# A buffer for x's second part, a later start for pairs 3 to 10, and w_out's sums in thirds of one tile

## The chip, the cores and the metric

One core of a Trainium2 chip. The metric is the device time of one execution, in microseconds; lower is better.

## What is computed

```python
q_n, k_n = rmsnorm(q, g_q), rmsnorm(k, g_k)            # q, k, v: 8 batches x 12 heads x 448 x 64
scores = q_n @ k_n.T / sqrt(64);  scores -= scores.max(-1)
attn = exp(scores) / (exp(scores).sum(-1) + 1e-9)
x = heads_side_by_side(attn @ v)                       # 3584 x 768
h = x @ w_in                                           # 768 x 2048
g = s * maximum(h, 0) ** 2 + b
return g @ w_out                                       # 2048 x 768, result 3584 x 768, float32
```

The weights arrive as 64-bit words; the kernel makes float32 of them itself.

## The kernel before

**Order.** Every engine runs its instructions in the order in which the program issues them: a block switches the scheduler off for all engines, so the order is written by hand. SP issues nearly all DMAs, one after the other; a DMA that waits for a buffer or for data holds up all that stands behind it on SP.

**Attention** works on 48 pairs of heads. A pair has four pieces, each a slot (192 slots, and negative ones for the start). `slot(i)` issues the scores and the maxima due there, the transposed scores and the exponent of piece i, and then a list of jobs. `STAGES` (L30) says in which slot a pair's jobs are issued: an offset, and a tuple with the slots of the first pairs. The jobs: `load` brings raw q and k rows (L192, 448 KB, two buffers, on SP for pairs 0 to 3, on ACT's queue later); `norm` squares on ACT (L198), sums on DVE (L203, ssq), and takes the power −1/2 on POOL (L205, L206, ri); `keep` writes these factors to memory (L209, i_d); `load_kq` brings k, q and v (L215, kqv, 704 KB); `spread` reads i_d back as a broadcast (L222, rb, two buffers); `scale` multiplies by g on ACT (L229) and by rb on POOL (L233, DVE for half of pair 0), and three slots later casts to kr (ACT L238). Then `score` (PE L247, sh), `maximum` (DVE L256, nmx), `shift` (SP L265, shq), `score_t` (PE L276, and L280 with shq), `exponent` (ACT L287, e), `weigh` (PE L297, L304) and `take` (ACT L319, L320). A tail per pair fetches the sums (L323, L327), inverts them (L331), writes them (L336, z_d), reads them as a broadcast (L341, uz), divides on POOL (L347) and writes x (L350). `convert` brings w_in's words (L356) and makes float32 sums of them on the side.

**FFN.** Both products are done in blocks of 2 x 2 with seven products of sums instead of eight. x is read in parts: `s_load` (SP L449) into a tile of nine (tag s9, two pools of one buffer each), `s_sums` (POOL L137 to L139), `s_split` (ACT cast L149, DVE subtraction L151) into tags s0, s1, s2. Three parts, s_0 to s_2, are needed by the first product, `ffn_in` (PE L483, 63 matmuls a block, 56 blocks n); they are issued among attention's last slots, in program order for SP, POOL, ACT and DVE alike. `rectify` empties a block's banks (ACT L494 to L497, DVE L492) and writes r_d (L527). Beside blocks 2 to 50, `convert_out` makes sums of w_out in 32 steps, two for each k from 0 to 15: a load (L575), the words (ACT L110, DVE L111 to L118), sums on POOL; `keep_out` writes w_d (L593). The sums stand in a tile of nine, odd k under 12 in a pool with two buffers (w9), all others in a single buffer (o9). `tout_load` (L560) brings seven of them back, two buffers from w9; `tout_split` (L149, L151) makes the high and the low part for the last stage, `multiply` (PE L657).

```python
            if k % 2 and k < 12:
                o9s[k] = pools["w9"].tile([P, 9, HC], F32, tag="w9", bufs=2, name=f"o9_{k}")
            else:
                o9s[k] = pools["c"].tile([P, 9, HC], F32, tag="o9", name=f"o9_{k}")
```

Of the kernel before, what the change touches and what calls it, by code (L numbers as in the profile page):

```python
# [9 lines left out]
F32 = mybir.dt.float32  # L10
# [17 lines left out]
AHEAD = 10  # L28

STAGES = {  # L30
    "raw": (-21, (-14, -14, -12, -11, -8, -5, -2, 0, 2)),
    "norm": (-16, (-13, -12, -10, -7, -4, -1, 1, 3)),
    "keep": (-13, (-11, -9, -7, -4, -2, 1, 3)),
    "kq": (-8, (-12, -8)),
    "spread": (-10, (-10, -9, -6, -3, 0, 2)),
    "scale": (-5, (-9, -5, -2, 1, 3, 6)),
}


# [6 lines left out]
def attention_then_relu2_ffn(  # L46
# [17 lines left out]
    NPAIR, P, _, TILES, D = kq_rows.shape  # L64
# [10 lines left out]
    NSLOT = W * NPAIR  # L75
# [17 lines left out]
    HC = HALF // 2  # L93
    TG = 4 * P
    NG = NT // TG
    QUADS = 4
# [70 lines left out]
    def attention(ps):  # L167
# [212 lines left out]
        def at(slot, f, *a):  # L380
            jobs[slot].append((f, a))
# [15 lines left out]
            at(s0 + 20, put_x, p)  # L397
        at(FIRST, constants)
        for n in range(NM * NK):
            at(8 + 27 * n // 4, convert, n)  # L400

        def slot(i):
            if i == FIRST:
# [36 lines left out]
    def s_load(n):  # L440
        u, k = divmod(n, NK)
        g = min(u, 2 * NG - 2 - u)
        t = s9s[n] = pools["s9", n % 2].tile([P, 9, 2 * P], F32, tag="s9", name=f"s9_{n}")
        t0 = TG * g
        while t0 < TG * (g + 1):
            b, off = divmod(t0, SEQ)
            w = min(TG * (g + 1) - t0, SEQ - off)
            o = t0 - TG * g
            nc.sync.dma_start(  # L449
                four(t, 2 * P)[:, :, o : o + w],  # L450
                x_d[b][2 * k : 2 * k + 2, :, off : off + w].rearrange("f p t -> p f t"),
            )
            t0 += w
# [10 lines left out]
    def finish(g):  # L464
        for _ in g:
            pass
# [95 lines left out]
    def tout_split(k):  # L562
        m, h = divmod(k, 2)
        to, c = t_out(m), slice(h * HC, (h + 1) * HC)
        return split((to[:, 0, :, c], to[:, 1, :, c]), tls.pop(k))

    o9s = {}

    def convert_out(n):
        k, nh = divmod(n, 2)  # L570
        m, h = divmod(k, 2)
        w = pools["c"].tile([P, 2, HC, 2], I32, tag="c64", bufs=2, name=f"w64o{n}")
        c0 = 2 * (nh * HALF + h * HC)
        src = w_out32[2 * m * P : 2 * (m + 1) * P, c0 : c0 + 2 * HC]
        nc.sync.dma_start(  # L575
            w.rearrange("p h n t -> p h (n t)"), src.rearrange("(h p) n -> p h n", h=2)
        )
        yield
        if nh == 0:
            if k % 2 and k < 12:  # L580
                o9s[k] = pools["w9"].tile([P, 9, HC], F32, tag="w9", bufs=2, name=f"o9_{k}")
            else:
                o9s[k] = pools["c"].tile([P, 9, HC], F32, tag="o9", name=f"o9_{k}")
        t = o9s[k]
        yield from words_of(
            t[:, nh : nh + 8 : 7].bitcast(I32), (w[:, :, :, 0], w[:, :, :, 1]),
            t[:, 2 + 2 * nh : 4 + 2 * nh],
        )
        if nh:
            sums_right(t, G)  # L590
# [100 lines left out]
    with tc.manual_schedule(engines=ORDERED):  # L691
        lp = ctx.enter_context(tc.tile_pool(name="lpool", bufs=1))
        ap = early.enter_context(tc.tile_pool(name="apool", bufs=1))
        aps = early.enter_context(tc.tile_pool(name="aps", bufs=1, space=PSUM))
        slot = attention(aps)
        for i in range(FIRST, NSLOT + 3):
            slot(i)
            if i == NSLOT - 10:
                first.close()
                pools["s", True] = pools["s9", 0] = pools["s9", 1] = pool(mid, "spool", "right")  # L700
            for n in range(NK):
                if i == NSLOT - (10, 9, 6)[n]:
                    s_load(n)
                if i == NSLOT - (8, 6, 4)[n]:
                    s_sums(n)
                if i == NSLOT - (7, 5, 3)[n]:
                    finish(s_split(n))
        early.close()
        pools["w9"] = pools["t4"] = pool(ctx, "w9pool", "left")
        pools["c"] = pools["s9", 1] = pool(late, "cpool2", "left")  # L710
        pools["s", False] = pool(mid, "spool2", "right")
        ps = ctx.enter_context(
            tc.tile_pool(name="ps", bufs=1, space=PSUM, reuse_waits="tile")
        )
        todo = list(range(4 * NM))
        runs = [(g, 0) for g in range(NG)] + [(g, QUADS) for g in reversed(range(NG))]
        blocks = [(r, g, q0 + i) for r, (g, q0) in enumerate(runs) for i in range(QUADS)]
        nb = len(blocks)

        def fresh_x(r):  # L720
            return r + 1 < len(runs) and r != NG - 1

        def sums(n):

            r, _, q = blocks[n]
            if fresh_x(r):
                for k in {1: (0, 1), 2: (2,)}.get(q % QUADS, ()):
                    s_sums(first_s(r + 1) + k)

        def parts(n):  # L730

            r, _, q = blocks[n]
            if fresh_x(r):
                for k in {1: (0,), 3: (1, 2)}.get(q % QUADS, ()):
                    finish(s_split(first_s(r + 1) + k))
            b = n - (NG - 1) * QUADS
            if -2 <= b <= 0:
                for k in range(2):
                    tin_load(2 * (b + 2) + k)
            if 0 < b <= QUADS:  # L740
                for k in range(NK):
                    finish(tin_split(NK * (b - 1) + k))
                    tin_load(NK * (b + 1) + k)
            if n == nb - 14:
                tout_load(0)
                tout_load(1)
            if n == nb - 13:
                finish(tout_split(0))
                finish(tout_split(1))
            b = n - (nb - QUADS)  # L750
            if b == 0:
                tout_load(2)
                tout_load(3)
            elif b > 0:
                for k in (2 * b, 2 * b + 1):
                    finish(tout_split(k))
                    tout_load(k + 2)

        for n, (r, g, q) in enumerate(blocks):
            ffn_in(r, q)  # L760
            i = q % QUADS
            if fresh_x(r):
                for k in {0: (0, 1), 2: (2,)}.get(i, ()):
                    s_load(first_s(r + 1) + k)
            last, next_ = begun[:], []
            begun.clear()
            if n >= 2 and todo and i != 2 and not 24 <= n < 28:
                x = todo.pop(0)
                c = convert_out(x)
                next(c)  # L770
                next_.append(c)
                if x % 2 and x > 1:
                    keep_out(x // 2 - 1)
            sums(n)
            if n:
                rectify(*blocks[n - 1])
            for u in range(3 * n, 3 * n + 3):
                if u < 20:
                    slot(NSLOT + 3 + u)
            for x in last:  # L780
                finish(x)
            begun.extend(next_)
            parts(n)
            if n == nb - QUADS - 1:
                assert not todo and not begun
                keep_out(2 * NM - 1)
                late.close()
                pools["g"] = pool(ctx, "gpool", "left")
                for x in range(3):
                    g_load(x)  # L790
            if n == nb - 3:
                g_sums(0)
                g_sums(1)
            if n == nb - 2:
                g_load(3)
                g_load(4)
        g_split(0)
        mid.close()
        pools["t"] = pool(ctx, "tpool", "right")
        rectify(*blocks[-1])  # L800
        g_split(1)
        g_sums(2)
        for k in (8, 9):
            finish(tout_split(k))
            tout_load(k + 2)
        for x in range(ROUNDS):
            g_load(x + 5)
            g_sums(x + 3)
            p, m = divmod(x, NM)
            if m < NM - 1:  # L810
                g_split(x + 2)
            for k in {0: (10, 11), 1: (12,), 2: (13,), 3: (14,), 4: (15,)}.get(x, ()):
                finish(tout_split(k))
                if k < 14:
                    tout_load(k + 2)
            if x < ROUNDS - 2:
                multiply(x)
            elif x == ROUNDS - 1:
                multiply(x - 1, x)
            if m == NM - 1:  # L820
                combine(p)
                g_split(x + 2)
            if m == 1 and p:
                store(p - 1)
# [42 lines left out]
```

## Time and profile before

| | |
|---|---|
| median of three runs | 1416.88 us (1413.33 to 1419.38) |
| the profiled execution, time | 1416.61 us |
| its span | 1414.8 us |
| TensorE (PE) busy | 1342.3 us, 95% |
| VectorE (DVE) | 1001.4 us, 71% |
| ScalarE (ACT) | 779.5 us, 55% |
| GpSimd (POOL) | 824.1 us, 58% |
| mean granted clock of TensorE | 0.978 |

Attention takes the span's first 558 us, the first product runs to about 987, the second to the end. In each, TensorE is busy almost throughout; its idle time is gathered at the start, between the stages, and at a few places inside.

### The profile page before, as it was taken

The numbers are of one execution on the slowest core, as the hardware profiler recorded it, in microseconds if no ns is written. First come the engines' busy times: TensorE is split into PE (matmuls) and PEld (weight loads), VectorE is DVE, ScalarE is ACT, GpSimd is POOL, SyncE is SP. The second block draws the span as 40 slices with busy tenths as digits, with TensorE's granted clock in tenths as the row PEclk, the third lists the DMA queues.
The fourth block names the chain that finished last, engine by engine and source line by source line (L and its number), as shares of the span: only waits on it lengthen the run. The fifth ranks groups of instructions, "written<-read, shape, count | busy, mean of one in ns | idle before, by whom it ended". The sixth has DMA issues, their size and how long they took to land.

```text
span 1414.8 us, 25920 instructions
## 1 busy us (share of the span) xinstructions
PE 1342.3 (95%) x9760; PEld 1068.7 (76%) x9760; DVE 1001.4 (71%) x1539; ACT 779.5 (55%) x1185; POOL 824.1 (58%) x714
## 2 busy tenths in 40 slices
PE   3699999999999996999999999899899999999999
PEld 2344444444444443999999999899799999999998
DVE  3467767776666631789888886777977766777666
ACT  3467767766666652333435332435665665656654
POOL 5468988877878623656544445260455655455553
PEclk6799999999999998999999999999999999999999
DMA  6578898889899813556567566457533332233231
GB/s 212 163 194 228 243 234 257 233 256 263 239 268 262 238 57 113 177 188 207 183 230 251 173 199 207 160 186 248 200 98 110 107 98 90 90 118 99 98 96 61
DMA packets 170733, 252.12 MB, mean 178 GB/s; under 512 B 53680, under 2 KB 121200, under 8 KB 170608
## 3 DMA queue, kind: packets, MB, share of 16 engines
q1 hardware_dynamic: 164272, 230.29, 52.7%
q10 hardware_dynamic: 6336, 20.19, 5.2%
q8 instruction: 76, 1.25, 0.4%
q14 instruction: 49, 0.40, 0.1%
HBM read 181.49 MB, written 68.76 MB: 177 GB/s over the span
## 4 chain that ended last, share of the span: by engine, by line
PE 74%; DMA 8%; DVE 6%; issue 4%; POOL 3%; ACT 3%; SPq 1%; ACTq 0%; DVEq 0%; POOLq 0%
PE m L657 27%; PE h L483 21%; PE av L297 9%; PE st L276 8%; PE av L304 4%; PE sh L247 4%; DMA uz<-z_d 2%; PE st L280 2%; DMA to<-w_d 2%; DVE r L492 1%; DMA i_d<-ri 1%; DVE s L151 1%; DVE nmx L256 1%; ACT s L149 1%; DMA w_d<-o 1%
## 5 line engine op out<-in xcount | busy, mean ns | idle before, releaser
L483 PE MATMUL h<-s,tin 128*128 128x256 f32 x3528 | 423.8, 283 | 5.4 <-DVE r L492 4.2
L483 PEld LDWEIGHTS h<-s,tin 128*128 128x128 f32 x3528 | 422.1, 190 | 8.0 <-DVE r L492 5.7
L657 PE MATMUL m<-tout,gh 128*128 128x384 f32 x1568 | 403.3, 338 | 3.3 <-ACT gh L641 3.1
L256 DVE TENSOR_REDUCE nmx<-sh 112x2 fp32r<-112x896 f32 x192 | 209.1, 1090 | 144.3 <-PE sh L247 141.4
L657 PEld LDWEIGHTS m<-tout,gh 128*128 128x128 f32 x1568 | 285.8, 189 | 4.7 <-ACT gh L641 3.7
L657 PE MATMUL m<-tout,gl 128*128 128x384 f32 x784 | 265.7, 339 | 5.0 <-DVE gl L642 5.0
L287 ACT ACTIVATE e<-st 128x896 f32<-128x896 f32 x192 | 176.7, 922 | 118.1 <-PE st L280 117.8
L621 POOL TENSOR_TENSOR g<-g 128x256 f32<-128x256 f32 x112 | 94.6, 845 | 218.7 <-DVE g L620 218.7
L276 PE MATMUL st<-kqv 64*128 64x448 f32 x768 | 181.6, 550 | 8.3 <-ACT e L287 8.3
L642 DVE TENSOR_TENSOR gl<-g,gh 128x896 fp32r<-128x896 f32 x112 | 138.1, 1233 | 62.6 <-ACT gh L641 62.4
L297 PE MATMUL av<-e,kqv 128*32 128x448 f32 x1536 | 166.2, 551 | 11.2 <-ACT uz L320 7.2
L641 ACT CAST gh<-g 128x896 fp32r<-128x896 f32 x112 | 105.5, 942 | 111.2 <-POOL g L625 59.9
L657 PEld LDWEIGHTS m<-tout,gl 128*128 128x128 f32 x784 | 148.4, 189 | 6.9 <-DVE gl L642 6.9
L233 POOL TENSOR_TENSOR kqv<-kqv,rb 128x448 f32<-128x448 f32 x95 | 122.7, 1306 | 49.6 <-ACT kqv L229 19.6
L492 DVE TENSOR_TENSOR r<-r,h 128x256 f32<-128x256 f32 x408 | 139.4, 413 | 12.6 <-ACT r L496 12.4
L280 PE MATMUL st<-shq,row 64*128 64x448 f32 x384 | 141.0, 726 | 4.8 <-DMA shq<-nmx 4.8
L247 PEld LDWEIGHTS sh<-kr 64*112 64x112 f32 x384 | 54.4, 278 | 115.9 <-issue 29.3
L206 POOL TENSOR_TENSOR ri<-ri,mhalf 128x14 f32<-128x14 f32 x48 | 138.9, 2893 | 4.0
L625 POOL TENSOR_TENSOR g<-g 128x256 f32<-128x256 f32 x112 | 135.6, 1211 | 0.0
L151 DVE TENSOR_TENSOR s<-s,s 128x1792 fp32r<-128x1792 f32 x39 | 82.0, 2108 | 57.1 <-ACT s L149 56.6
L247 PE MATMUL sh<-kr 64*112 64x448 f32 x384 | 92.5, 478 | 29.4 <-ACT kr L238 19.7
L149 ACT CAST s<-s 128x1792 fp32r<-128x1792 f32 x39 | 66.0, 1696 | 81.0 <-POOL s L139 48.1
(78 smaller groups left out, 1604.2 us busy)
## 6 DMA issues: line engine op xcount, KB each, us to landing
kqv<-in_dram SPq DMA_DIRECT2D x48, 704.0 KB
raw<-r_d SPq DMA_DIRECT2D x112, 256.0 KB
r_d<-r SPq DMA_DIRECT2D x51, 512.0 KB
rb<-i_d SPq DMA_DIRECT2D x96, 224.0 KB
raw<-in_dram ACTq DMA_DIRECT2D x44, 448.0 KB
w64i<-in_dram SPq DMA_DIRECT2D x24, 512.0 KB
w64o<-in_dram SPq DMA_DIRECT2D x32, 384.0 KB
uz<-z_d SPq DMA_DIRECT2D x96, 112.0 KB
```

What stands on the lines that cost most here:

```text
L206: G.tensor_tensor(ri, ri, mhalf[:, :n], ALU.pow)
L247: T.matmul(sh[:QC, j, :SEQ], t[d, 1].rearrange("k (p c) -> k c p", c=NQ)[:, c], t[d, 0], start=True, stop=True,)
L256: V.tensor_reduce(out=nmxs[p][:, :, c : c + 1], in_=shs.pop(i)[:QC, :, :SEQ], op=ALU.max, axis=AX.X, negate=True,)
L276: T.matmul(st[:, j, :SEQ], t[d, 0, k0 : k0 + P], t[d, 1], start=True, stop=False)
L280: T.matmul(st[:, j, :SEQ], row[d], shq[p % 3][d], start=False, stop=True)
L287: S.activation(e, sts.pop(i)[:, :, :SEQ], AF.Exp)
L297: T.matmul(t[n * Q : (n + 1) * Q, 0, :SEQ], x[:, 2 * g + h, j, m * Q : (m + 1) * Q], e[h][:, j], start=g + h == 0, stop=g + h == 2,)
L483: T.matmul(to, w[:, lw, sa], x[:, lx, tb], start=k == n == 0 and j % 2 == 0, stop=k == NK - 1 and n == 2, skip_group_check=True,)
L492: V.tensor_tensor(to, a, part(j), op_)
L625: G.tensor_tensor(g9[:, 5:7], g9[:, 0:9:8], g9[:, 1:8:6], ALU.subtract)
L642: V.tensor_tensor(gl, g9[:, 1:8], gh.bitcast(F32), ALU.subtract)
L657: T.matmul(to, g[:, sa], w, start=m == 0 and n == 0, stop=m == NM - 1 and n == 2,)
```

## The change

Three parts. **The start:** `STAGES` issues the kqv of pair 0 before the second raw, and moves load, powers, i_d and rb of pairs 3 to 10 to later slots; w_in's conversions begin in slot 14 instead of 8, the last begins in slot 163 as before. **The end of attention:** s_load(1) uses the place of tag s2, where the result of part 2 will go, instead of the s9 buffer that part 0 used; loads, sums and splits of parts 1 and 2 are issued in other slots. **w_out:** for k from 8 on, the sums stand in one of three thirds of a tile `spare`, which takes the place (tag t0) that `staged` had and `tout0` will have; below 8, odd k use w9 and even ones o9. The first two tout loads move from block 42 to block 50, their splits from 43 to 52.

```diff
 STAGES = {
-    "raw": (-21, (-14, -14, -12, -11, -8, -5, -2, 0, 2)),
-    "norm": (-16, (-13, -12, -10, -7, -4, -1, 1, 3)),
-    "keep": (-13, (-11, -9, -7, -4, -2, 1, 3)),
-    "kq": (-8, (-12, -8)),
-    "spread": (-10, (-10, -9, -6, -3, 0, 2)),
-    "scale": (-5, (-9, -5, -2, 1, 3, 6)),
+    "raw": (-21, (-14, -14, -12, -9, -5, 0, 2, 4, 6, 8)),
+    "norm": (-16, (-13, -12, -10, -2, -1, 2, 4, 6, 8, 10)),
+    "keep": (-13, (-11, -9, -7, 0, 2, 4, 6, 9, 11)),
+    "kq": (-8, (-14, -12, -6, -1, 1, 3)),
+    "spread": (-10, (-10, -8, -6, 0, 3, 4, 7, 10)),
+    "scale": (-5, (-9, -4, -2, 1, 4, 6)),
 }
...
-            at(8 + 27 * n // 4, convert, n)
+            at(14 + 13 * n // 2, convert, n)
...
-        t = s9s[n] = pools["s9", n % 2].tile([P, 9, 2 * P], F32, tag="s9", name=f"s9_{n}")
+        tag = "s2" if n == 1 else "s9"
+        t = s9s[n] = pools["s9", n % 2].tile([P, 9, 2 * P], F32, tag=tag, name=f"s9_{n}")
...
-            if k % 2 and k < 12:
+            if k >= 8:
+                if not spare:
+                    spare.append(pools["t4"].tile([P, 3, 9, HC], F32, tag="t0", name="spare"))
+                o9s[k] = spare[0][:, k % 3]
+            elif k % 2:
...
-                if i == NSLOT - (10, 9, 6)[n]:
+                if i == NSLOT - (10, 9, 5)[n]:
                     s_load(n)
-                if i == NSLOT - (8, 6, 4)[n]:
+                if i == NSLOT - (8, 6, 3)[n]:
                     s_sums(n)
-                if i == NSLOT - (7, 5, 3)[n]:
+                if i == NSLOT - (7, 4, 1)[n]:
                     finish(s_split(n))
...
-            if n == nb - 14:
+            b = n - (nb - QUADS)
+            if b == -2:
                 tout_load(0)
                 tout_load(1)
-            if n == nb - 13:
-                finish(tout_split(0))
-                finish(tout_split(1))
-            b = n - (nb - QUADS)
-            if b == 0:
-                tout_load(2)
-                tout_load(3)
-            elif b > 0:
+            if b >= 0:
                 for k in (2 * b, 2 * b + 1):
                     finish(tout_split(k))
                     tout_load(k + 2)
```

What moves at the start, on SP, from its first transfer to the first shift. A number behind a name counts the program's tiles; raw_373 is pair 0's in both, i_d_275 to i_d_279 belong to pairs 0 to 4. Before:

```order
L192 DMA raw_373<-in_dram 128x896
L192 DMA raw_375<-in_dram 128x896
L157 DMA gg<-in_dram 128x2
L215 DMA kqv_385<-in_dram 128x1408
...
L215 DMA kqv_427<-in_dram 128x1408
L222 DMA rb_429<-i_d_277 64x896 x2
L209 DMA i_d_278<-ri_424 128x14
L215 DMA kqv_453<-in_dram 128x1408
L222 DMA rb_455<-i_d_278 64x896 x2
L209 DMA i_d_279<-ri_450 128x14
L265 DMA shq_343<-nmx_440 1x112x4 x2
```

After:

```order
L192 DMA raw_373<-in_dram 128x896
L215 DMA kqv_375<-in_dram 128x1408
L192 DMA raw_377<-in_dram 128x896
L157 DMA gg<-in_dram 128x2
...
L209 DMA i_d_277<-ri_404 128x14
L215 DMA kqv_419<-in_dram 128x1408
L222 DMA rb_421<-i_d_277 64x896 x2
L265 DMA shq_343<-nmx_429 1x112x4 x2
```

gg stands behind a kqv as well, and the first shift stands directly behind the rb of pair 2, no longer behind i_d, kqv and rb of pair 3 and i_d of pair 4.

On DVE the same stretch, before:

```order
L203 TENSOR_REDUCE ssq_402<-raw_388 128x14
L233 TENSOR_TENSOR kqv_385<-kqv_385,rb_398 128x448
L203 TENSOR_REDUCE ssq_422<-raw_396 128x14
L256 TENSOR_REDUCE nmx_440<-sh_437 112x2
L256 TENSOR_REDUCE nmx_440<-sh_444 112x2
L203 TENSOR_REDUCE ssq_448<-raw_416 128x14
L256 TENSOR_REDUCE nmx_440<-sh_458 112x2
L256 TENSOR_REDUCE nmx_440<-sh_470 112x2
```

After:

```order
L203 TENSOR_REDUCE ssq_402<-raw_390 128x14
L233 TENSOR_TENSOR kqv_375<-kqv_375,rb_398 128x448
L256 TENSOR_REDUCE nmx_429<-sh_426 112x2
L256 TENSOR_REDUCE nmx_429<-sh_434 112x2
L256 TENSOR_REDUCE nmx_429<-sh_438 112x2
L256 TENSOR_REDUCE nmx_429<-sh_446 112x2
L203 TENSOR_REDUCE ssq_452<-raw_411 128x14
```

The sums of squares of pairs 3 and 4 have left the four maxima of pair 0.

ACT at the end of attention, from the cast of s_0 on (e are the exponents of slots 186 on, sz and uz what `take` copies). Before:

```order
L149 CAST s_5591<-s_0_5523 128x1792
L287 ACTIVATE e_5599<-st_5594 128x896
L287 ACTIVATE e_5613<-st_5608 128x896
L149 CAST s_5629<-s_1_5547 128x1792
L287 ACTIVATE e_5637<-st_5632 128x896
L287 ACTIVATE e_5652<-st_5647 128x896
L319 COPY sz_5670<-av_5616 128x448
L320 COPY uz_5669<-av_5616 128x448
L149 CAST s_5673<-s_2_5605 128x1792
L287 ACTIVATE e_5681<-st_5676 128x896
L287 ACTIVATE e_5689<-st_5684 128x896
```

After:

```order
L149 CAST s_5591<-s_0_5523 128x1792
L287 ACTIVATE e_5599<-st_5594 128x896
L287 ACTIVATE e_5610<-st_5605 128x896
L287 ACTIVATE e_5634<-st_5629 128x896
L149 CAST s_5641<-s_1_5547 128x1792
L287 ACTIVATE e_5649<-st_5644 128x896
L319 COPY sz_5667<-av_5613 128x448
L320 COPY uz_5666<-av_5613 128x448
L287 ACTIVATE e_5678<-st_5673 128x896
L287 ACTIVATE e_5686<-st_5681 128x896
L149 CAST s_5702<-s_2_5626 128x1792
```

The cast of s_1 stands one exponent later, that of s_2 behind the last two.

SP in the first product near block 42, before:

```order
L527 DMA r_d_3_113<-r_5_9770 128x2x512
L560 DMA to_9790<-w_d_0_259 128x1344
L560 DMA to_9792<-w_d_1_260 128x1344
L575 DMA w64o_9861<-in_dram 128x2x384
L593 DMA w_d_0_271<-o_12_9591 128x1344
```

After, the same place and then the new place of the two loads:

```order
L528 DMA r_d_3_113<-r_5_9766 128x2x512
L576 DMA w64o_9852<-in_dram 128x2x384
L598 DMA w_d_0_271<-spare 128x1344
...
L528 DMA r_d_1_111<-r_5_10520 128x2x512
L561 DMA to_10534<-w_d_0_259 128x1344
L561 DMA to_10536<-w_d_1_260 128x1344
L528 DMA r_d_1_118<-r_6_10605 128x2x512
```

The write of the sums now comes from a third of `spare`, and the loads of the last stage's first two parts come some eight blocks later.

## Rows read from the trace of the kernel before

**Rows 1.** Windows: stretch, length, PE PEld DVE ACT POOL busy (instructions), PEclk, DMA share, GB/s.

```profile
2.00:4.00 2.00, 2.00 (x10) 2.00 (x11) 0.00 (x0) 0.20 (x1) 0.53 (x2) 1.00 0.89 330
...
0.00:35.00 35.00, 12.13 (x56) 9.32 (x56) 13.74 (x20) 10.74 (x13) 20.31 (x24) 0.70 0.70 213
...
400.00:500.00 100.00, 98.69 (x788) 45.75 (x790) 66.36 (x90) 66.99 (x92) 74.88 (x64) 1.00 0.85 249
530.00:570.00 40.00, 26.58 (x193) 16.64 (x192) 9.37 (x20) 11.35 (x15) 15.73 (x15) 0.87 0.37 110
...
880.00:920.00 40.00, 35.71 (x270) 34.27 (x269) 28.48 (x51) 14.90 (x29) 9.68 (x10) 0.94 0.53 173
```

**Rows 2.** Chain of waits at the start: start, length, what.

```profile
1.62 4.56 DMA gg<-in_dram
...
13.37 5.97 DMA i_d<-ri
...
27.81 6.50 DMA i_d<-ri
...
36.18 2.91 DMA shq<-nmx
```

**Rows 3.** Timeline of the start: start, length, engine, line, operation [idle before].

```profile
7.77 2.61 POOL L206 TENSOR_TENSOR ri<-ri,mhalf 128x14 f32<-128x14 f32 x1
...
19.19 1.47 POOL L233 TENSOR_TENSOR kqv<-kqv,rb 128x448 f32<-128x448 f32 x1 [2.88 <-DMA rb<-i_d]
...
21.68 1.85 PE L247 MATMUL sh<-kr 64*112 64x448 f32 x8 [12.60 <-ACT kr L238]
...
22.45 2.09 DVE L256 TENSOR_REDUCE nmx<-sh 112x2 fp32r<-112x896 f32 x2 [1.74 <-PE sh L247]
...
39.13 0.90 PE L280 MATMUL st<-shq,row 64*128 64x448 f32 x2 [4.78 <-DMA shq<-nmx]
```

**Rows 4.** Timeline of attention's end, PE, DVE, SP, POOL and ACT.

```profile
525.29 1.02 PE L276 MATMUL st<-kqv 64*128 64x448 f32 x4
...
527.39 1.71 PE L297 MATMUL av<-e,kqv 128*32 128x448 f32 x16
...
529.79 1.02 PE L276 MATMUL st<-kqv 64*128 64x448 f32 x4
...
528.01 2.02 DVE L151 TENSOR_TENSOR s<-s,s 128x1792 fp32r<-128x1792 f32 x1 [11.35 <-ACT s L149]
...
530.06 0.87 SPq L449 DMA_DIRECT2D s<-x_d  x2
...
535.79 1.13 POOL L347 TENSOR_TENSOR uz<-uz 128x448 f32<-128x448 f32 x1 [12.52 <-DMA uz<-z_d]
...
540.07 1.68 ACT L149 CAST s<-s 128x1792 fp32r<-128x1792 f32 x1 [10.47 <-POOL s L139]
...
542.62 1.87 PE L276 MATMUL st<-kqv 64*128 64x448 f32 x4 [8.26 <-ACT e L287]
...
553.13 3.05 PE L297 MATMUL av<-e,kqv 128*32 128x448 f32 x16 [4.04 <-ACT e L287]
...
558.40 11.77 PE L483 MATMUL h<-s,tin 128*128 128x256 f32 x97 [1.11 <-ACT uz L320]
```

**Rows 5.** First product: chain of waits (first two rows), then timeline of DVE and PE.

```profile
558.40 291.29 PE h L483 x2453
...
879.58 8.10 DMA w_d<-o
...
887.77 0.36 DVE L111 TENSOR_SCALAR o<-w64o 128x384 int32<-128x384 int32 x1 [11.80 <-DMA w_d<-o]
...
896.41 3.02 DVE L151 TENSOR_TENSOR tout<-to,tout 128x1344 fp32r<-128x1344 f32 x2
...
890.36 25.23 PE L483 MATMUL h<-s,tin 128*128 128x256 f32 x189 [2.76 <-DVE r L492]
917.04 69.41 PE L483 MATMUL h<-s,tin 128*128 128x256 f32 x567 [1.45 <-DVE r L492]
```

More of the change, by code (lines that the diff above doesn't have):

```diff
@@ L565, in tout_split @@
         return split((to[:, 0, :, c], to[:, 1, :, c]), tls.pop(k))
-    o9s = {}
+    o9s, spare = {}, []
     def convert_out(n):
```

## The prediction

> **What bounds the kernel now.** I read the page first: TensorE is busy for 95% of the span, so of 1414.8 us only some 70 can be won without less matmul work. Then the windows by stage [rows 1] say where those are: between 400 and 500 us PE is busy for 98.69 of 100, but for only 12.13 of the first 35, for 26.58 of the 40 from 530 (attention ends, the FFN begins), and for 35.71 of the 40 from 880. The change touches these three places, so each is one term. In each I looked up what released PE after its idle time (the timeline), and what that thing had waited for (the chain of waits).
>
> The sum is made against the profiled run's 1416.61 us, 1414.8 of span and 1.8 around it; the median of the runs shown is 1416.88, 0.27 above. Differences under 0.5%, about 7 us, are what a measurement of this kernel can't tell from no change.
>
> **Term A, the start.** Before, first scores start at 21.68, the first matmul with the shift row (L280) at 39.13, 4.78 idle, and from there the pairs follow each other at PE's own order, which is the same in both kernels. So the term is how early L280 can start. The new chain, link by link:
>
> - gg. It landed 4.56 us after its issue [rows 2], though it is 1 KB. Now the first kqv, 704 KB, is ahead of it, and the queue moved 330 GB/s there [rows 1]: 704 KB by that is 2.2 us. DVE's g product, behind which the sums of squares stand, moves from 6.2 to 8.4. The Trainium skill (DMA: Bandwidth & Descriptors, section on queues, rings and completion order) says that each DMA engine takes the descriptors of a ring in ring order; gg's late landing agrees. By that rule the sum below stands; were gg free to pass, the start would be 2.2 us earlier and the whole 1382.3.
> - Powers. The first ends at 7.77 + 2.61 = 10.38 [rows 3]; 2.2 later is 12.6. Three follow each other at 2.98 (the small op and gaps included), so POOL is free at 18.5. Before, it then stood until 19.19 for the broadcast row rb. The new rb is issued after the first i_d, near 14, and has neither raw of pair 3 ahead of it nor raw of pair 4 beside it. The 4.5 from there are above the 2.91 of a shift [rows 2], so I let it land by 18.5.
> - Scale and cast: 21.68 − 19.19 = 2.49 [rows 3], so first scores at 21.0. Before, maxima of the first pair had the sums of squares of pairs 3 and 4 among them, and these waited for their loads. Now four stand back to back at 2.09 / 2 = 1.05 each [rows 3]: done near 26.
> - The shift. Before, SP issued it at 36.18, behind waits for i_d of 5.97 and 6.50 [rows 2] among others. Now the rows of pairs 3 and 4 stand behind it, so it is issued when the maxima end or when the rb of pair 2 is out, 26 to 28, and lands 2.91 later [rows 2]: 29 to 31. Two scores of pair 1 stand before it on PE. Their i_d, issued at 15.6 with the second power, lands with rb near 19, their rb 4 later; two halves scaled on POOL (1.1 each without DVE beside it), a cast of 0.9 and the scores at the lower clock, 1.5, give 28 as well, and L276 ahead of L280 1.5 more.
>
> So L280 starts near 30.5 instead of 39.13: 8.6 gained. The cast of pair 2 or 3 now stands behind an exponent and a scale on ACT, at worst 0.85 for one of each: **8 us** stays. Ends: if the new rb comes 2.2 later than the old, as gg does, the scores start at 21.68 + 2.2 = 23.9; if then each i_d takes 6 again, pair 1's scores and L280 end up at 34.8, and 2 more go at pairs 3 and 4, whose loads are now late: 2. If no link waits and some small gaps after 40 go too: 11. I take the value near the short ends because what stood ahead in the queue is what is moved.
>
> The w_in conversions begin 6 slots later and end at the same slot; POOL and DVE have room there, since PE is the bound in that stretch [rows 1]: nothing.
>
> **Term C, the end of attention.** PE stops at 534.36 for 8.26 until 542.62, then 4.04 before 553.13, then 1.11 before 558.40, where the FFN's first product starts [rows 4]. The 8.26 is an exponent that stands on ACT behind the cast of s_1 at 540.07, and that waited for POOL's sums. Why were these late? SP's load of s_1 was issued at 530.06, as soon as DVE's subtraction for s_0 (528.01 + 2.02) gave the buffer back. Behind this waiting load stands SP's get of z, so POOL's division at 535.79 had waited 12.52 us for it, and POOL's sums of s_1 stood behind the division. Now s_1 is loaded into another buffer and waits for nothing: load near 518, division and sums done by 529, cast when its slot comes. It is put after the exponent of slot 188, and that of s_2 after the last exponent, so no exponent is behind a cast that waits. s_2's load takes over the wait at 530; behind it on SP stand a put and a get for pairs that only the tail needs.
>
> What is then left of PE's work after 534.36: two slots of scores with what lies between, 529.79 − 525.29 = 4.50, the last weighing, 529.79 − 527.39 = 2.40, and 1.11 that I leave: 542.4 instead of 558.40. The stalls also cost the clock (0.87 in that window [rows 1]); this is in the difference, since the 4.50 is at full clock. **16 us.** s_2 must then be there 5 us into the product (it is used in the last third of 63 matmuls), so by 547: load 530, 4 to landing (between the 2.91 of the shift and the 4.56 of gg [rows 2]), sums 3.1 (from the division's end at 536.92 to the cast), cast 1.7, subtraction 2, so 541. Ends: only the second stall goes, 4; all goes, with the 1.11, 17.
>
> **Term D, the w_out sums.** PE's pace in these products is 291.29 / 2453 = 0.1187 us a matmul [rows 5]. It waits 2.76 before 890.36 and 1.45 before 917.04; the 189 after the first took 25.23 where the pace gives 22.4, and the 567 after the second 69.41 where it gives 67.3, the clock of that stretch being 0.94 [rows 1]. That is 2.76 + 1.45 + 2.8 + 2.1 = 9.1. The cause: DVE's conversion (887.77) had waited 11.80 for the write of the previous sums (8.10 in flight) to leave the single buffer, and PE's banks are emptied by DVE behind it. Three thirds of one tile make the wait two conversions long, so it is gone. The two loads and splits of w_out's first parts move by some 9 blocks; their 3.02 of DVE [rows 5] now lie beside the next ones, in the last four blocks. There they push the next two loads by 1 to 2 us, and the first rounds of the last stage live on these; I charge 1. **8 us**, ends 2 and 10.
>
> Sum: 8 + 16 + 8 = 32; 1416.6 − 32 = 1384.6, given as **1384.5**. By the ends, 1378.6 to 1408.6; that all three hit the same end is unlikely.
>
> **Rivals.**
> - R1: the start gains nothing, because gg, powers and i_d waits add what the moved rows save. For it: each link is on the chain, and gg comes later. Against: first scores were set by rb, not by gg. 1392.6, chance 0.13.
> - R2: term D is handed back in the last four blocks, where the splits collide with the emptying of banks and the two-buffer loads. For it: the splits are moved to the busiest place for DVE. 1392.6, chance 0.12.
> - R3: the change does not do what it says at the end of attention: the division waits for z anyway, s_1's sums stay late, only 4 of 16 comes. For it: z's path is four transfers long. Against: its get was issued behind the waiting load. 1396.6, chance 0.05.
> - R4, the other side: pairs 3 to 10 starve. Their load, powers, i_d, rb and scale begin only after the first pair's maxima, and SP's wait for i_d, 5.4 to 6.5 us [rows 2], is no longer covered by the time bought at the start. Uncovered for 8 pairs it is 47: 1416.6 − 24 + 47 = 1439.6. It is slower by more than 0.5% from (24 + 7) / 8 = 3.9 us uncovered a pair. Against it: a pair keeps PE busy for 9 to 10 us, and a pair's whole chain runs beside others. Chance 0.05, 0.03 of it beyond that point.
>
> **How the numbers follow.** The forecast has 0.65, its own range 1377 to 1391. The range goes on to 1399 to take in R1, R2, R3 and the low ends of a term. All but R4 are faster by over 0.5%: 0.95; a milder R4 is the 0.02 for no change, and 0.03 is slower.
>
> **What would show it.** Right: the first exponent near 31 instead of 40; first scores near 21; no idle of 8.26 and 4.04 on PE at the end of attention, and the FFN's first product near 534 (558.4 − 24); no DVE wait for a write of w_d, no PE wait for DVE between 880 and 920 of before; granted clock 1.00 in both stretches. Wrong: PE idle before the scores of pairs 3 to 6, released by ACT's cast, would be R4 in part; a division that still waits over 10 us would be R3; new idle time in the last blocks or first rounds of the last stage would be R2.

## The result, and the profile after

The changed kernel takes 1393.26 us (median of four, 1392.45 to 1396.16); the kernel before took 1418.13 beside it (median of four). The ratio is 0.9833, 95% interval 0.9803 to 0.9863: 24.9 us won, where 32 had been forecast. The time lies inside the range given, 1377 to 1399, and outside the forecast's own 1377 to 1391. The profiled execution has a span of 1391.4 us.

Windows of the changed kernel (stretch, length, busy time of PE, PEld, DVE, ACT, POOL with instructions, granted clock, DMA share, GB/s); the third and the fourth are the places of the 530 and 880 windows [rows 1], 15.6 and 20 us earlier:

```profile
0.00:35.00 35.00, 12.12 (x58) 9.85 (x60) 12.36 (x19) 9.59 (x12) 18.92 (x23) 0.70 0.57 188
400.00:500.00 100.00, 97.53 (x782) 45.06 (x782) 65.63 (x91) 67.30 (x93) 75.26 (x63) 1.00 0.86 247
514.40:554.40 40.00, 38.89 (x327) 21.75 (x326) 12.39 (x21) 20.88 (x28) 17.90 (x16) 1.00 0.45 124
860.00:900.00 40.00, 40.00 (x340) 40.00 (x339) 33.38 (x60) 14.55 (x28) 21.92 (x18) 1.00 0.58 195
```

The end of attention and the first product are full now, 38.89 of 40 and 40 of 40 at clock 1.00. The start is not: 12.12 of 35 as before. And in the window from 400 to 500, which the change only touches by the conversions, PE is busy for 1.2 less.

What ended PE's idle time, in the changed kernel (engine, line, releaser: us in total, times, longest):

```profile
PE sh L247 <- ACT kr L238: 21.4, 4, 11.7
PE av L297 <- ACT uz L320: 10.6, 13, 2.0
PE sh L247 <- DVE nmx L256: 9.5, 10, 1.3
```

Before, the first and the second of these were 19.7 and 7.2. The exponents (8.3 and 4.0), the shift row (4.8) and DVE's rectifying (4.2), all among the waits before, are gone.

To see where the time went I cut each profiled execution at the same instructions: PE's first L280, ACT's cast of kr for the eighth pair (the expectations call it pair 8) and for the last pair, the first matmul of the first FFN product, the first matmul of the last stage, the end. All times are in us.

| us | kr of pair 1 | L280 | eighth cast | eighth to last cast | to first product | first product to last stage | rest | span |
|---|---|---|---|---|---|---|---|---|
| before | 28.70 | 39.13 | 94.34 | 409.39 | 54.67 | 429.14 | 427.28 | 1414.8 |
| changed | 29.84 | 34.08 | 90.40 | 413.91 | 38.49 | 420.77 | 427.78 | 1391.4 |
| difference | +1.1 | −5.1 | −3.9 | +4.5 | −16.2 | −8.4 | +0.5 | −23.5 |

So the end of attention gave the 16 of term C, the first product and the last stage together 7.9 of term D's 8. By the eighth pair the start had given 3.9 instead of 8, and the 40 pairs after it, where I had put nothing, were 4.5 longer.

**The start.** Timeline of the changed kernel (start, length, engine, line, operation, idle before and its releaser):

```profile
9.44 2.61 POOL L206 TENSOR_TENSOR ri<-ri,mhalf 128x14 f32<-128x14 f32 x1
...
18.21 1.47 POOL L233 TENSOR_TENSOR kqv<-kqv,rb 128x448 f32<-128x448 f32 x1 [0.22 <-DMA rb<-i_d]
...
20.05 0.43 SPq L215 DMA_DIRECT2D kqv<-in_dram  x1
20.55 0.66 ACT L229 ACTIVATE kqv<-kqv,gqk 128x448 f32<-128x448 f32 x1
20.70 1.85 PE L247 MATMUL sh<-kr 64*112 64x448 f32 x8 [11.65 <-ACT kr L238]
21.47 4.09 DVE L256 TENSOR_REDUCE nmx<-sh 112x2 fp32r<-112x896 f32 x4 [2.74 <-PE sh L247]
23.11 2.12 POOL L233 TENSOR_TENSOR kqv<-kqv,rb 128x448 f32<-128x448 f32 x2 [3.44 <-DMA rb<-i_d]
...
26.32 1.23 SPq L265 DMA_DIRECT2D shq<-nmx  x2
...
28.43 0.67 ACT L229 ACTIVATE kqv<-kqv,gqk 128x448 f32<-128x448 f32 x1 [7.21 <-DMA kqv<-in_dram]
29.00 0.93 ACT L198 ACTIVATE raw<-raw 128x896 f32<-128x896 f32 x1
...
29.84 0.92 ACT L238 CAST kr<-kqv 128x896 fp32r<-128x896 f32 x1
...
30.82 0.73 PE L247 MATMUL sh<-kr 64*112 64x448 f32 x2 [8.27 <-ACT kr L238]
...
34.08 1.25 PE L280 MATMUL st<-shq,row 64*128 64x448 f32 x2
```

The chain that I had followed from [rows 3] came as forecast (forecasts in brackets): scores at 20.70 (21.0), four maxima back to back, over at 25.56 (26), the shift issued at 26.32 (26 to 28). But POOL had pair 1 scaled at 25.23, and its cast only started at 29.84: ACT stood for 7.21 us at L229, pair 2's scaling by g, for a kqv that SP had issued at 20.05. That L229 now stands ahead of the cast; before, the cast of pair 1 was ahead of it. ACT in the kernel before, pair 1's cast and then pair 2's scaling:

```profile
28.70 0.94 ACT L238 CAST kr<-kqv 128x896 fp32r<-128x896 f32 x1 [0.80 <-POOL kqv L233]
...
29.55 0.66 ACT L229 ACTIVATE kqv<-kqv,gqk 128x448 f32<-128x448 f32 x1
```

L280 no longer waited for the shift: PE came to it at 34.08 without idle time, behind the scores of pair 1 and L276.

**The end of attention**, against [rows 4]:

```profile
518.73 0.95 SPq L450 DMA_DIRECT2D s<-x_d  x2
...
525.57 1.13 POOL L347 TENSOR_TENSOR uz<-uz 128x448 f32<-128x448 f32 x1 [1.40 <-DMA uz<-z_d]
...
532.53 1.68 ACT L149 CAST s<-s 128x1792 fp32r<-128x1792 f32 x1
...
542.80 418.92 PE L484 MATMUL h<-s,tin 128*128 128x256 f32 x3528 [1.11 <-ACT uz L320]
```

Part 1 is loaded at 518.73, the division waits 1.40 instead of 12.52, the cast of s_1 follows an exponent directly. The last row is also the whole first product: 3528 matmuls without a gap.

### The profile page after: what moved, and what is told of

It is laid out like the page before. It is cut to its first block, busy times and chain, and to the rows that moved or that the text cites. A ratio compares the mean times of both kernels' runs of the same rounds, so it can differ in the third digit from the quotient of the medians.

```text
span 1391.4 us, 25928 instructions
## 1 busy us (share of the span) xinstructions
PE 1334.7 (96%) x9760; PEld 1065.0 (77%) x9760; DVE 1008.1 (72%) x1539; ACT 780.4 (56%) x1185; POOL 830.7 (60%) x714
## 4 chain that ended last, share of the span: by engine, by line
PE 78%; DMA 10%; DVE 4%; POOL 3%; issue 3%; ACT 2%; SPq 1%; ACTq 0%; DVEq 0%; POOLq 0%
PE h L484 28%; PE m L662 27%; PE av L297 8%; PE st L276 7%; PE av L304 3%; PE sh L247 3%; PE st L280 2%; DMA w64i<-in_dram 1%; DMA kqv<-in_dram 1%; DMA x_d<-uz 1%; DMA to<-w_d 1%; DMA uz<-z_d 1%; DMA rb<-i_d 1%; DVE nmx L256 1%; POOL kqv L233 1%
## 5 line engine op out<-in xcount | busy, mean ns | idle before, releaser
L484 PE MATMUL h<-s,tin 128*128 128x256 f32 x3528 | 418.9, 281 | 1.1 <-ACT uz L320 1.1
L276 PE MATMUL st<-kqv 64*128 64x448 f32 x768 | 180.7, 547 | 0.0
L297 PE MATMUL av<-e,kqv 128*32 128x448 f32 x1536 | 164.2, 545 | 10.6 <-ACT uz L320 10.6
L233 POOL TENSOR_TENSOR kqv<-kqv,rb 128x448 f32<-128x448 f32 x95 | 128.5, 1369 | 36.4 <-DMA rb<-i_d 11.7
L280 PE MATMUL st<-shq,row 64*128 64x448 f32 x384 | 141.1, 728 | 0.0
L137 POOL TENSOR_TENSOR s<-s 128x512 f32<-128x512 f32 x39 | 55.7, 1428 | 85.0 <-DMA s<-x_d 53.5
```

The source lines that it names most:

```text
L233: E.tensor_tensor(of, of, rb[:, n], ALU.mult)
L276: T.matmul(st[:, j, :SEQ], t[d, 0, k0 : k0 + P], t[d, 1], start=True, stop=False)
L280: T.matmul(st[:, j, :SEQ], row[d], shq[p % 3][d], start=False, stop=True)
L297: T.matmul(t[n * Q : (n + 1) * Q, 0, :SEQ], x[:, 2 * g + h, j, m * Q : (m + 1) * Q], e[h][:, j], start=g + h == 0, stop=g + h == 2,)
L484: T.matmul(to, w[:, lw, sa], x[:, lx, tb], start=k == n == 0 and j % 2 == 0, stop=k == NK - 1 and n == 2, skip_group_check=True,)
```

## The experiments

There are twelve runs of ten kernels; each is the changed kernel with the edit shown, and two kernels ran a second time ("the same again"). The table cuts their profiled executions as above; ratios are of timed runs, against the kernel before on the same chip.

| | kr of pair 1 | L280 | eighth cast | eighth to last | to product | product | rest | median us | ratio (95%) |
|---|---|---|---|---|---|---|---|---|---|
| old conversions | 30.35 | 34.59 | 90.94 | 410.02 | 38.49 | 422.47 | 427.92 | 1391.31 | 0.9817 (0.9786 to 0.9849) |
| old stages | 29.95 | 40.13 | 94.51 | 417.15 | 38.49 | 421.85 | 427.51 | 1393.72 | 0.9846 (0.9804 to 0.9888) |
| kqv of pair 2 first | 28.34 | 32.59 | 88.96 | 415.38 | 38.49 | 421.03 | 427.82 | 1390.37 | 0.9810 (0.9778 to 0.9842) |
| this, and old conversions | 28.38 | 32.62 | 88.98 | 407.30 | 38.49 | 420.85 | 427.85 | 1387.21 | 0.9799 (0.9769 to 0.9828) |
| the same again | 27.33 | 31.58 | 88.57 | 412.03 | 38.50 | 422.63 | 427.03 | 1385.39 | 0.9775 (0.9749 to 0.9801) |
| and cast ahead | 24.81 | 29.15 | 87.10 | 413.47 | 38.49 | 420.79 | 427.82 | 1388.80 | 0.9791 (0.9769 to 0.9813) |
| the same again | 25.16 | 29.42 | 85.83 | 408.24 | 38.51 | 421.56 | 427.74 | 1388.79 | 0.9792 (0.9766 to 0.9818) |
| one s9 | 29.37 | 33.61 | 89.82 | 415.72 | 49.31 | 422.71 | 427.49 | 1404.40 | 0.9894 (0.9867 to 0.9920) |
| old slots | 29.08 | 33.32 | 89.53 | 415.60 | 40.26 | 421.08 | 427.63 | 1394.63 | 0.9822 (0.9788 to 0.9855) |
| no spare | 28.44 | 32.69 | 89.57 | 417.68 | 38.49 | 421.61 | 428.14 | 1394.59 | 0.9832 (0.9809 to 0.9855) |
| no spare, loads early | 29.95 | 34.19 | 90.07 | 409.02 | 38.49 | 428.64 | 427.94 | 1397.02 | 0.9859 (0.9830 to 0.9889) |
| spare, loads early | 28.90 | 33.14 | 89.30 | 410.01 | 38.49 | 421.52 | 427.94 | 1394.11 | 0.9834 (0.9801 to 0.9868) |

**Do the conversions cost the middle, from the eighth to the last cast, its 4.5?** Two kernels, one with each half of the first part undone.

```diff
-            at(14 + 13 * n // 2, convert, n)
+            at(8 + 27 * n // 4, convert, n)
```

> The changed kernel, with w_in's conversions in their old slots (8 + 27n/4). In the changed kernel the cast of kr for pair 8 came 3.94 us earlier than before, that for the last pair 0.58 us later: 4.5 lost in the middle of attention. Theory 'conversions' (their new slots cost that 4.5): the last cast comes near 500 instead of 504.3, PE's idle time in attention's middle falls by some 4, and the span from 1391.4 to about 1387. Rival 'queue' (the middle is paced by transfers on SP's queue, and gives back whatever the start gained): no change, last cast at 504 +- 1, span 1391 +- 1.5.

The middle took 410.02 and the last cast came at 500.96: what 'conversions' asked for. PE's waits for the copies of av in that stretch are 10.6 in the changed kernel and 6.4 here. The other half, the old table with the new slots of the conversions:

> The changed kernel, with the old table of stages, the new slots of the conversions kept. Theory 'conversions': the start loses its 4 to 5 us and the middle loses its 4.5 too, last cast near 508, span near 1396. Rival 'queue': the start is later, at L280 39.1 instead of 34.1, but the middle gives nothing back, last cast again near 504, span near 1391.

L280 fell back to 40.13, the eighth cast to 94.51, so the new table is worth 4.1 there. The middle did not give it back: 417.15, last cast 511.66. The median, 1393.72, is the same as that of the changed kernel. The timed runs of the kernel with old stages lie between 1388.90 and 1401.31, and in such a spread what the start gains can't be seen. That the new table makes the kernel faster is shown for the start of the profiled executions, not for the time.

**Is pair 1's cast held by the load of pair 2?** SP's two transfers changed round:

```diff
-    "raw": (-21, (-14, -14, -12, -9, -5, 0, 2, 4, 6, 8)),
+    "raw": (-21, (-14, -14, -12, -7, -5, 0, 2, 4, 6, 8)),
-    "kq": (-8, (-14, -12, -6, -1, 1, 3)),
+    "kq": (-8, (-14, -12, -9, -1, 1, 3)),
```

> The changed kernel, with two transfers on SP changed round: kqv of pair 2 where raw of pair 3 stood, ahead of the broadcast for pair 1, and raw of pair 3 behind i_d of pair 2. Theory 'cast behind a load' (pair 1's cast stood on ACT for 4.6 us behind pair 2's scaling by g, which waited for kqv until 28.4): that cast starts near 26 instead of 29.84, L280 near 30.3 instead of 34.08, and the span is some 3.8 shorter, 1387.6, if the middle keeps it. Rival 'the shift' (its landing near 29 and pair 1's own broadcast set L280 anyway): L280 not before 33.5, span within 1 of 1391.4. By 'queue' L280 is early but the last cast stays at 504.

Only 1.5 came, L280 at 32.59, between what the theory and its rival asked for. The wait had moved to another instruction. ACT's rows in this kernel:

```profile
21.41 0.67 ACT L229 ACTIVATE kqv<-kqv,gqk 128x448 f32<-128x448 f32 x1 [0.72 <-DMA kqv<-in_dram]
...
27.49 0.95 ACT L198 ACTIVATE raw<-raw 128x896 f32<-128x896 f32 x1 [5.41 <-DMA raw<-in_dram]
28.34 0.92 ACT L238 CAST kr<-kqv 128x896 fp32r<-128x896 f32 x1
```

L229 now waits 0.72, but the next instruction ahead of the cast, the square of pair 3, waits 5.41 for the raw that I had moved back.

> Both edits, kqv of pair 2 first and the conversions in their old slots. By 'conversions' with 'cast behind a load' the two add up: L280 near 30.3, last cast near 496.5, span near 1383.5. By 'queue' L280 is early and the last cast at 503 to 504, span 1391. With only one theory right, 1387.

1387.21, last cast at 496.29, span 1383.5, as if both had added up. Then the square of pair 3 was put behind the cast, by one slot:

```diff
-    "norm": (-16, (-13, -12, -10, -2, -1, 2, 4, 6, 8, 10)),
+    "norm": (-16, (-13, -12, -10, -1, -1, 2, 4, 6, 8, 10)),
```

> Kqv of pair 2 first and the conversions in their old slots, and norm of pair 3 one slot later. In the kernel without this last edit pair 1's cast started at 28.34, though POOL had scaled at 25.2: ACT stood at the square of pair 3, whose raw landed at 27.49. Theory 'cast behind a load': the cast now starts near 25.3, scores of pair 1 at 26.3, L280 at 29.5 (behind the shift's landing at 28), 3 earlier than 32.59, and the span goes from 1383.5 to 1380.5. Rival: pair 3's square is late in turn, kr of pair 3 starts later than 50.0 and PE waits there for what was won: span within 1 of 1383.5.

```profile
24.81 0.94 ACT L238 CAST kr<-kqv 128x896 fp32r<-128x896 f32 x1 [3.31 <-POOL kqv L233]
...
25.96 1.23 SPq L265 DMA_DIRECT2D shq<-nmx  x2
...
29.15 1.17 PE L280 MATMUL st<-shq,row 64*128 64x448 f32 x2
```

Here the theory held to 0.5 us: the cast (24.81) waits for POOL alone, L280 starts at 29.15. So what kept L280 from the 30.5 of the prediction was ACT, which takes its instructions in order and stood at one that waited for a load: L229 in the changed kernel, the square of pair 3 when L229 no longer had to wait. That is shown. But the span was 1387.7, not 1380.5. By the eighth cast 1.9 of the 3.5 were left, and the middle took 413.47, with the old slots of the conversions. That spoke against 'conversions', so this kernel and the one before it ran again, side by side on one chip.

> The kernel with kqv of pair 2 first and the conversions in their old slots, once more, beside the next. From the cast of pair 8 to the last cast, kernels with old conversion slots took 409.4, 410.0, 407.3 and 413.5 and those with new slots 413.9, 417.2, 415.4, 415.7, 415.6 and 417.7. Theory 'conversions': below 412 here. If the two groups only differ by chance: anywhere from 407 to 418.

> The kernel with pair 1's cast ahead of pair 3's square, once more. Its middle took 413.5, the longest with old conversion slots. Theory 'queue in part' (what the start wins beyond a few us is given back where transfers pace the middle): again 412 to 415, and the time within 0.2% of the kernel beside it. If that was chance: 407 to 411, span near 1381, and 2 to 3 faster than the one beside it.

One program took 407.30 and 412.03 in the middle, the other 413.47 and 408.24: single executions of one kernel differ by 5 us there. And the last two kernels of the table, with the new slots, took 409.02 and 410.01. With the six executions in old slots (407.3 to 413.5, mean 410.1) and eight in new ones (409.0 to 417.7, mean 414.3), the new slots may cost about 4. The medians point the same way, 1391.31 against 1393.26 and 1387.21 against 1390.37, with intervals that overlap. But the groups overlap, and the 4.5 is no larger than the spread of one program. The chip is a rival too: on that of the first four kernels old slots took 407.30 and 410.02 and new ones 415.38 and 417.15, on the next an old one 413.47 and new ones 415.60 to 417.68, on that of the two repeated runs and the last two kernels old ones 408.24 and 412.03 and new ones 409.02 and 410.01. The two executions of each program were on different chips as well. **This stays open.** What is shown is the place: nearly all of PE's idle time there is its wait for ACT's copies of av. It is 10.6 in the changed kernel, and it goes with the length: 4.9 in the execution of 407.30, 9.1 in that of 412.03 of the same program. Near 448 us the chain of the changed kernel shows what one such copy stood behind, the tail's transfers:

```profile
435.24 6.41 DMA zt<-s_d
...
441.71 6.18 DMA x_d<-uz
...
448.80 0.55 ACT uz L320
```

The DMA share is 0.86 in the window from 400 to 500. 'Queue' falls as it was put, since the last casts do not come at a common time (494.07 to 511.66). 'Queue in part' does not: the second profile of cast ahead kept its lead (middle 408.24, span 1381.9), but in the medians this kernel is not faster than the one beside it (1388.79 against 1385.39, intervals overlapping). So its last 3 us at the start are not shown in the time.

**What made the end of attention 16 shorter?** First the buffer undone, then the slots.

```diff
-        tag = "s2" if n == 1 else "s9"
+        tag = "s9"
```

> The changed kernel, with x's part 1 back in the s9 buffer that part 0 uses; the new slots kept. From the last cast of kr to the first FFN product it took 54.67 before, 38.49 in the changed kernel and 38.49 to 38.50 in four kernels with this part of the change. Theory 'buffer' (SP stands at this load, and the get of z behind it makes the division and POOL's sums late): the load is issued near 531 instead of 518.7, the division again waits over 10, an exponent waits 7 to 8 behind the cast of s_1, and the stretch takes 46 to 50; with part 2 then late for the product, 8 to 12 longer in all. Rival 'slots' (the later slots of casts and sums did it): 38.5 to 40.

Timeline of this kernel, SP, POOL, ACT and PE:

```profile
531.87 0.87 SPq L450 DMA_DIRECT2D s<-x_d  x2
...
537.27 1.13 POOL L347 TENSOR_TENSOR uz<-uz 128x448 f32<-128x448 f32 x1 [12.08 <-DMA uz<-z_d]
...
541.56 1.68 ACT L149 CAST s<-s 128x1792 fp32r<-128x1792 f32 x1 [7.69 <-POOL s L139]
...
544.11 1.87 PE L276 MATMUL st<-kqv 64*128 64x448 f32 x4 [6.79 <-ACT e L287]
```

The links of [rows 4] are back as far as the first stall: the load at 531.87, the division's wait of 12.08, and 6.79 on PE for an exponent, where it was 8.26. The stretch is 49.31, the time 1404.4, 11 more than the changed kernel. The second stall of [rows 4], 4.04, is not back. Now the other half, the slots:

```diff
-                if i == NSLOT - (10, 9, 5)[n]:
+                if i == NSLOT - (10, 9, 6)[n]:
-                if i == NSLOT - (8, 6, 3)[n]:
+                if i == NSLOT - (8, 6, 4)[n]:
-                if i == NSLOT - (7, 4, 1)[n]:
+                if i == NSLOT - (7, 5, 3)[n]:
```

> The changed kernel, with the old slots of loads, sums and splits of x's parts at the end of attention; part 1 stays in the place of s2. 'Buffer': sums of part 1 are done in time, no stall there; part 2's cast is again ahead of the last two exponents, and waits for a load that can't be issued before 530, so 2 to 4 of idle PE: the stretch from last cast to first product 40.5 to 42.5. 'Slots': back to 50 or more.

Timeline of this kernel, PE:

```profile
541.76 1.77 PE L297 MATMUL av<-e,kqv 128*32 128x448 f32 x16 [1.50 <-ACT e L287]
```

The stretch is 40.26, 1.8 more, by an idle time of 1.50 behind the cast of s_2; 40.5 to 42.5 and 2 to 4 of idle time had been expected. So the buffer is worth 10.8 with the new slots and 14.4 with the old ones, the slots 1.8 with the buffer and 5.4 without it; without either, the second stall is there too.

**What made the first product 8 shorter?** The sums back in their old buffers, late loads kept:

```diff
-            if k >= 8:
-                if not spare:
...
-                o9s[k] = spare[0][:, k % 3]
-            elif k % 2:
+            if k % 2 and k < 12:
```

> The changed kernel, with w_out's sums for k from 8 on in the old buffers (odd k under 12 in w9, all others in the single one); the first loads and splits of the last stage stay at blocks 50 and 52. From the first product's start to the last stage's start it took 429.14 before, 420.77 in the changed kernel. Theory 'single buffer' (DVE's conversion waits for the write of the sums before): 428 to 429, DVE waits over 8 for the write of w_d, PE waits for DVE twice. Rival 'places' (before, the first two loads of the last stage stood on SP just ahead of that write): 421 to 422 here too.

A miss for 'single buffer': 421.61, within the 420.77 to 422.71 of the kernels with the spare tile, and PE without a gap. DVE still waited for the write, but 7.42 instead of 11.80 [rows 5], and PE did not stop for it. The write itself was 4.64 in flight, not 8.10 (first row from the chain of waits, second from the timeline):

```profile
865.69 4.64 DMA w_d<-o
...
870.46 0.36 DVE L111 TENSOR_SCALAR o<-w64o 128x384 int32<-128x384 int32 x1 [7.42 <-DMA w_d<-o]
```

So the place of the loads matters, as the rival said. Two more kernels have the first two loads back at block 42 (splits stay at 52), one without the spare tile, one with it:

```diff
-            if b == -2:
+            if n == nb - 14:
                 tout_load(0)
                 tout_load(1)
```

> The kernel without the spare tile (sums in the old buffers), with the first two loads of the last stage back at block 42, their splits kept at block 52. Without the spare tile but with late loads, the first product had taken 421.61, no worse than with it, and DVE had waited 7.42 for the write of w_d, against 11.80 before. Theory 'write behind loads' (before, the write stood on SP behind two loads of 688 KB, was 8.10 in flight, and only that made DVE's wait longer than PE's banks could cover): DVE waits over 10 again, PE waits for DVE, the stretch from first product to last stage takes 427 to 430. Rival 'splits' (their 3 us of DVE and 2.6 of ACT among the first product's blocks cost it): 421 to 423.

The chain of waits of this kernel has the write:

```profile
857.05 8.94 DMA w_d<-o
```

and its timeline SP, DVE and PE:

```profile
854.66 1.33 SPq L561 DMA_DIRECT2D to<-w_d  x2
...
857.05 0.45 SPq L594 DMA_DIRECT2D w_d<-o  x1
...
866.09 0.36 DVE L111 TENSOR_SCALAR o<-w64o 128x384 int32<-128x384 int32 x1 [11.85 <-DMA w_d<-o]
...
868.68 46.98 PE L484 MATMUL h<-s,tin 128*128 128x256 f32 x378 [1.89 <-DVE r L493]
...
966.22 1.01 PE L658 MATMUL m<-tout,gh 128*128 128x384 f32 x2 [4.29 <-ACT gh L642]
```

The write, behind two loads of 672 KB (688 in thousands of bytes, as the expectation has it) on the same queue, is 8.94 in flight; DVE waits 11.85, PE stops, and the stretch takes 428.64. So the write's delay and PE's stop come back with the loads. They are not the whole of the loss before, although the stretch is nearly as long (429.14): up to its last matmul the product takes 424.4 here, 418.9 in the changed kernel and 428.1 in the kernel before, so 5.4 of 9.1 are back. The rest of the stretch is the wait of 4.29 before the last stage, which is 1.85 to 3.71 in the kernels with this part whole. The kernel before also had the splits at block 43; what they carried of the other 3.7, no run shows. With the spare tile and the same early loads:

> The changed kernel with the spare tile, with the first two loads of the last stage back at block 42. 'Write behind loads': the write is late again, but the next conversion has another third and doesn't wait: 421 to 422.5 from first product to last stage, so each of the two edits of this part is enough alone. If the loads cost by their transfers or in another way: 425 or more.

421.52, and no DVE wait for a write. So each of the two edits of this part is enough alone, and the two together give no more than one. In the medians the last two kernels are only 2.9 apart (1397.02 and 1394.11, intervals overlapping), as the middle differs from execution to execution; what is shown is the stretch.

## Why the prediction was right or wrong

- **The sum.** 32 forecast, 24.9 measured in the medians, 23.5 between the profiled executions. The sign, the range and two of three terms held. The failure is in term A and in the "nothing" beside it, and of the signs named in advance two failed by it: the first exponent came at 35.41, not near 31, and the first product at 542.80, not near 534. The time lies within 1 us of R1's 1392.6, but not for R1's reasons: the start did gain, and what was lost went at pair 1's cast and in the middle.
- **gg and the powers: right.** gg's product moved from 6.21 to 7.88, 1.7 where 2.2 was worked out; the powers ended at 18.0 instead of 18.5. The rb was there, POOL waited 0.22 for it.
- **The shift: right.** Issued at 26.32.
- **"a cast of 0.9 and the scores at the lower clock, 1.5, give 28 as well": wrong, and the step that failed.** I took i_d, rb, POOL's scaling and the cast itself, and these came as summed (POOL was done at 25.23, the sum has 19 + 4 + 2.2 = 25.2). I left out what the change puts ahead of pair 1's cast on ACT, L229 of pair 2 behind the kqv issued at 20.05 and the square of pair 3; I had looked at ACT's order for pairs 2 and 3 only. It cost 4.6 (25.23 to 29.84), and with it L280 came at 34.08 instead of 30.5; with both out of the way it came at 29.15 and 29.42.
- **"from there the pairs follow each other at PE's own order": not quite.** From L280 to the eighth cast it took 55.2 before and 56.3 in the changed kernel, so 1.1 of the 5.1 was gone by then.
- **"The w_in conversions ...: nothing": not confirmed.** The middle was 4.5 longer in the profiled execution. The runs put about 4 on the new slots but don't settle it, since one program varies by 5 there. My reason, room on POOL and DVE, did not look at what PE waits for in that stretch: ACT's copies of av, and behind the one followed back, the tail's transfers.
- **Term C: right, in size and in cause.** 16.2 for 16, and 38.49 to 38.51 in all eleven profiled executions that had this part whole. That SP's waiting load held the get of z, and so the division, is shown by the kernel with one s9.
- **Term D: right in size, incomplete in cause.** Up to its last matmul the product is 9.1 shorter, as summed; 0.8 goes in a longer wait before the last stage and 0.5 in that stage, for the 1 that I charged. I named the single buffer and the 8.10 in flight, and did not ask why a write of 672 KB should take so long: two loads stood ahead of it on the queue, as SP's order around block 42 shows. Moving them, which I had entered as a cost of 1, would have been enough.
- **Rivals.** R1 (the start gains nothing) was half true, by a mechanism that I hadn't named. R2, R3 and R4 did not come: the wait before the last stage and the stage itself lost 1.3 together, the division waited 1.40, and PE had no idle time over 1.3 before the scores of pairs 2 to 6.

The kernel with kqv of pair 2 first and the conversions in their old slots had lower medians than both: 1387.21 and 1385.39, ratios 0.9799 and 0.9775 to the kernel before, where the changed kernel has 0.9833. The second of these intervals (0.9749 to 0.9801) lies just below that of the changed kernel (0.9803 to 0.9863), the first overlaps it.

## What to carry to other kernels

When a table of slots moves loads back, read the in-order queue of each engine just ahead of the instruction that PE waits for: an instruction of a later tile that waits for a load holds it as surely as a missing input. A DMA that waits for a buffer costs whatever stands behind it on its queue; at the end of attention another place to land, even a borrowed one, was worth 10.8 us, the new slots 1.8. Before a buffer is added for a slow transfer, look at what stands ahead of that transfer: moving it may be enough.

## What was not expected

One and the same program took 407.30 and 412.03, and another 413.47 and 408.24, for the same 40 pairs of attention, while the start up to them repeated to within 1.3 us and the end of attention to within 0.02. In the changed kernel DMA is busy for 0.86 of the window from 400 to 500, and the wait followed back there ends at two transfers (6.41 for zt, 6.18 for x). Whether the chip has a part in it, these runs do not show; but timed runs of one kernel on one chip differ as well, by 6 us (1384.39 to 1390.54) in one case and by 12 (1388.90 to 1401.31) in another. A difference of a few us in such a stretch can't be read from one profile of each kernel.
